# Two tokens per partition for the first pair of a linear-attention and MLP kernel, with its last tile put out in halves and its order drawn anew

## The chip, the core and the metric

The kernel runs on one core of one Trainium2 chip. The metric is the device time of one execution in microseconds (us). A profile is one execution whose instructions were recorded; its span goes from the first to the last instruction and is about 2 us shorter than the execution's time. Each execution also has its mean granted TensorE clock on record, as a share of full speed; in this case that number turned out to sort the runs better than their times do.

Runs are called slow here when they are over 1.5% above the fastest run of the same kernel, and fast otherwise. A run in which the clock fell for a short while can still count as fast by this rule.

## The reference, cut to what matters

```python
def _attn_ref(r, k, v, w, u):            # B=4, H=8, S=768, D=48, float32
    state = np.zeros((B, H, D, D))
    for t in range(S):
        cur = np.einsum('bhd,bhe->bhde', u[None] * kt, vt)
        y[:, :, t] = np.einsum('bhd,bhde->bhe', rt, state + cur)
        state = wt[:, :, :, None] * state + np.einsum('bhd,bhe->bhde', kt, vt)
    return y

def _moe_ref(x, w_in, w_out, s, b):      # 3072 tokens, 384 -> 2048 -> 384
    r = np.maximum(x @ w_in, 0.0)
    return (s * (r * r) + b) @ w_out
# x is y with its heads laid side by side: (B*S, H*D) = (3072, 384)
```

## The kernel before

The kernel cuts each of the four sequences into six chunks of 128 tokens, which gives 24 token tiles n. For each tile the recurrence is turned into matmuls: running sums of log w (`cum`, tile `cums`), their exponentials (`E`), the products of r and k with them (`prd`), a transpose (`trps` to `RK`), the products of all pairs of tokens (`mt_ps`, masked to `mt_sb`), the output `y_ps` (to `x_sb`) and the new state (`d_ps`). Two tiles of `x_sb`, transposed to `xT`, make one MLP tile T of 256 tokens: `h_ps`, a ReLU to `rh`, its square `gT`, then `o_ps`, `o_sb` and the store.

Head by head, one token of one input is 48 numbers, 192 B, in memory. So a load of one tile is 1,024 pieces of 192 B:

```python
    def coords(n):
        return n // B, n % B             # chunk, batch: first the first chunks of the four batches

    def load(n, which):                  # which: 0 w, 1 r, 2 k, 3 v
        cc, bb = coords(n)
        t0 = cc * L                      # L = 128
        # ... (a tile of ain, 8 buffers of each kind)
        nc.sync.dma_start(
            out=dst, in_=src[bb, :, t0 : t0 + L, :].transpose([1, 0, 2])
        )

    def cum(n):
        ps = psA.tile([128, 2, 512], FP32, name="cums", tag="A")    # one buffer, shared with mt_ps
        lw = c["lw"]
        nc.tensor.matmul(ps[:, 0, 0:HD], lhsT=tri_strict, rhs=lw[:, :, 0:D], start=True, stop=True)
        nc.tensor.matmul(ps[:, 1, 0:HD], lhsT=ntri_incl, rhs=lw[:, :, 0:D], start=True, stop=True)
        # ... (four matmuls of one column for the decay of the state)

    def ymm(n):
        ps = psB.tile([128, 512], FP32, name="y_ps", tag="B")       # two buffers
        # ... (four matmuls with the state, if there is one)
        for h in range(H):
            p, sg = divmod(h, 2)
            nc.tensor.matmul(
                ps[:, h * D : (h + 1) * D],
                lhsT=c["mt"][:, sg, p, :],
                rhs=c["vb"][:, h, :],
                # ...
            )

    def g2(T, q):                        # o_ps of the last tile T is taken from psH
        tt, part = divmod(q, 4)
        # ...
        for ft in range(part * 4, part * 4 + 4):
            nc.tensor.matmul(ps, lhsT=gT[T][:, ft, tt * 128 : (tt + 1) * 128],
                             rhs=w_out_sb[ft // FPP][:, ft % FPP, :],
                             start=(ft == 0), stop=(ft == FT - 1))
```

Every instruction stands where a long list puts it; each engine works through its own in that order. `+7` stands for seven warm-up matmuls on zeros (`warm_ps`), which have no use but to keep TensorE busy:

```
load0.0 load0.1 load_u load1.0 load0.2 ln0 load2.0 +13 cum0 load1.1 +1 u_mm exp0 load1.2 u_ev l20
# ...
l22 dmm1 exp3 sup1 rkp3 xev0 +5 mt2 ymm1 mul3 li2 yd1 cd2 +5 tr3 ci0 load4.0 l23 yev1 vb2@P msk2
+6 xtr1 tev3 rku3 lo0 xev1 +7 dmm2 yd2 mt3 cd3 g10.0 sup2 ci1@A li3 msk3 ymm2 g10.1 vb3 relu0.0
# ...
```

In it `li` and `lo` are loads of the pieces of w_in and w_out, `ci` and `co` their casts, `g1` is h_ps, `g2` is o_ps, `tr` and `xtr` are the transposes on TensorE. Tiles from DTK on have r and k, and from DTX on have x, transposed by the DMA instead; from DK2 and DX2 on every second tile has, too.

## Time and profile before

| | before |
|---|---|
| time, median of 3 runs | 192.97 us (192.77 to 193.01) |
| span of the profiled run | 191.46 us, clock 1.00 |
| first h_ps starts | 23.57 us |
| TensorE busy after that | 161.9 us |
| TensorE idle after that | 2.4 us |
| from the last matmul to the end | 3.58 us |

The last four rows add up to the span. They are how the kernel is read in all that follows: a start, in which the first two tiles of attention are made; a dense middle, in which only the amount of TensorE work and its idle time count; and a tail.

Beside the views that the prediction shows, two places of the profile of before are needed later. From its page, the totals of the engines (busy time, share of the span, number of instructions) and one row of the DMA issues (count, KB of each, median us from issue to landing):

```profile
PE 181.7 (95%) x1859; PEld 140.6 (73%) x1859; DVE 125.1 (65%) x188; ACT 143.8 (75%) x272; POOL 105.8 (55%) x131
...
wt<-in_w_dram SPq DMA_DIRECT2D x24, 192.0 KB, 4.4
```

A load of 192 KB lands 4.4 us after it was issued, in the median of 24; its own pieces take only about 1.0 us of that, the pitch at which such loads are issued.

And the last VectorE work in its timeline (start, length, instruction, how many):

```profile
187.27 1.27 DVE L639 SCALAR_TENSOR_TENSOR o_sb<-o_psh,s_bc,bconst 128x384 f32<-128x384 f32 x2 [3.72 <-PE o_psh L629]
```

Both halves of the last MLP tile come to VectorE at nearly the same time, and the second, of 384 columns, ends 0.65 us after the last matmul.

### The profile page before, as it was taken

What the parts mean: (1) busy time and instruction counts of PE and PEld (TensorE: products, weight loads), DVE (VectorE), ACT (ScalarE), POOL (GpSimd) and SP (SyncE); (2) the same over time, 40 slices, a digit from 0 to 9 for tenths busy, and PEclk for the clock granted to TensorE, in tenths of its full rate; (3) what the DMA queues carried; (4) which work ended last, traced back from release to release, by engine and by line L of the source; (5) the groups of instructions that cost most, each with busy time, mean ns of one, the idle gap of its engine ahead of it and who ended that gap; (6) DMA issues with size and microseconds to landing.
All of it is one profiled execution on the core that took longest, in us unless ns stands there. A gap on an engine that the chain in (4) does not pass through costs nothing.

```text
span 191.5 us, 4784 instructions
## 1 busy us (share of the span) xinstructions
PE 181.7 (95%) x1859; PEld 140.6 (73%) x1859; DVE 125.1 (65%) x188; ACT 143.8 (75%) x272; POOL 105.8 (55%) x131
## 2 busy tenths in 40 slices
PE   6987889997999999999999999999999989999992
PEld 4665678875678877787878788888877767888761
DVE  6377784456857938869788697846859597640032
ACT  3756597895879999798869889785695994478910
POOL 3587821516688479799955885546677543100000
PEclk9999999999999999999999999999999999999999
DMA  6999999997999999999999999699999965123022
GB/s 116 197 188 206 312 342 371 238 284 137 189 160 221 184 198 191 187 198 192 222 192 208 178 166 227 145 202 243 177 187 140 203 136 142 25 67 125 0 82 82
DMA packets 124312, 34.75 MB, mean 181 GB/s; under 512 B 119169, under 2 KB 122242, under 8 KB 124290
## 3 DMA queue, kind: packets, MB, share of 16 engines
q1 hardware_dynamic: 124290, 34.45, 92.8%
q8 instruction: 14, 0.23, 0.5%
q14 instruction: 8, 0.07, 0.1%
HBM read 25.17 MB, written 4.72 MB: 156 GB/s over the span
## 4 chain that ended last, share of the span: by engine, by line
PE 63%; SPq 17%; DMA 5%; ACT 4%; issue 4%; DVE 3%; POOL 1%; DVEq 0%
PE h_ps L591 24%; PE o_ps L629 24%; SPq L270 14%; DMA wi_st<-in_moe_w_in_dram 4%; PE mt_ps L427 3%; PE o_psh L629 3%; PE y_ps L464 2%; DMA vt<-in_v_dram 2%; PE d_ps L480 2%; PE y_ps L455 2%; DVE gT L616 1%; PE cums L326 1%; PE cums L329 1%; SPq L696 1%; PE trps L385 1%
## 5 line engine op out<-in xcount | busy, mean ns | idle before, releaser
L591 PE MATMUL h_ps<-xT,w_in 128*128 128x256 bf16 x576 | 77.8, 273 | 0.9 <-DVE w_in L687 0.6
L629 PE MATMUL o_ps<-w_out,gT 128*128 128x384 bf16 x352 | 69.7, 326 | 0.6 <-DVE o_sb L639 0.6
L604 ACT ACTIVATE rh<-h_ps 128x512 bf16<-128x512 f32 x96 | 56.4, 598 | 17.8 <-PE h_ps L591 17.1
L591 PEld LDWEIGHTS <-w_in 128*128 128x128 bf16 x576 | 61.0, 114 | 7.6 <-DVE w_in L687 0.7
L629 PEld LDWEIGHTS <-gT 128*128 128x128 bf16 x384 | 35.5, 98 | 18.4 <-issue 0.6
L614 ACT ACTIVATE gT<-rh 128x512 bf16<-128x512 bf16 x67 | 40.2, 629 | 0.5
L282 POOL TENSOR_TENSOR rkp<-rkt 128x384 f32<-128x384 f32 x24 | 30.3, 1262 | 17.7 <-DMA rkt<-in_k_dram 17.7
L439 DVE TENSOR_TENSOR mt_sb<-mt_ps,tri_strict 128x1024 bf16<-128x1024 f32 x24 | 29.2, 1218 | 9.0 <-PE mt_ps L427 8.9
L358 DVE TENSOR_TENSOR prd<-rkt,E 128x768 bf16<-128x768 f32 x24 | 26.8, 1116 | 7.1 <-DMA rkt<-in_k_dram 5.9
L313 POOL TENSOR_TENSOR yd<-vt,cd 128x384 bf16<-128x384 f32 x24 | 22.0, 916 | 8.4 <-DVE cd L307 8.4
L293 POOL TENSOR_TENSOR rku<-rkp,u_bc 128x384 f32<-128x384 f32 x24 | 25.4, 1060 | 1.9 <-DVE cd L307 1.4
L348 ACT ACTIVATE E<-cums 128x768 bf16<-128x768 f32 x24 | 19.5, 811 | 5.5 <-PE cums L334 3.3
L639 DVE SCALAR_TENSOR_TENSOR o_sb<-o_ps,s_bc,bconst 128x384 f32<-128x384 f32 x22 | 13.3, 610 | 12.8 <-PE o_ps L629 12.4
L494 DVE TENSOR_TENSOR x_sb<-y_ps,yd 128x384 bf16<-128x384 f32 x24 | 13.3, 553 | 11.1 <-POOL yd L313 4.7
L616 DVE TENSOR_TENSOR gT<-rh 128x512 bf16<-128x512 bf16 x29 | 16.8, 594 | 1.9 <-ACT rh L604 1.6
L277 ACT ACTIVATE logw<-wt 128x384 bf16<-128x384 f32 x24 | 12.4, 525 | 5.8 <-DMA wt<-in_w_dram 5.7
L531 POOL TENSOR_TENSOR st<-stmp,l 128x384 bf16<-128x384 bf16 x16 | 14.7, 917 | 2.3 <-DVE stmp L522 2.3
L307 DVE TENSOR_REDUCE cd<-rku 128x8 f32<-128x384 f32 x24 | 13.0, 544 | 3.5 <-POOL rku L293 3.4
L866 PE MATMUL warm_ps<-warm_sb 128*128 128x256 bf16 x84 | 13.2, 295 | 1.1 <-DVE warm_sb L844 1.1
L685 POOL CAST vb<-vt 128x384 bf16<-128x384 f32 x12 | 6.8, 563 | 11.9 <-DMA vt<-in_v_dram 11.9
L400 ACT COPY RK<-trps 128x1024 bf16<-128x1024 bf16 x10 | 10.2, 1016 | 2.7 <-PE trps L385 2.3
L372 POOL TENSOR_TENSOR l<-lam,par 128x8 f32<-128x8 f32 x20 | 6.9, 348 | 8.3 <-ACT lam L352 8.3
(58 smaller groups left out, 168.9 us busy)
## 6 DMA issues: line engine op xcount, KB each, us to landing
wt<-in_w_dram SPq DMA_DIRECT2D x24, 192.0 KB, 4.4
rkt<-in_r_dram SPq DMA_DIRECT2D x24, 192.0 KB, 4.3
rkt<-in_k_dram SPq DMA_DIRECT2D x24, 192.0 KB, 4.3
vt<-in_v_dram SPq DMA_DIRECT2D x24, 192.0 KB, 4.2
out_dram<-o_sb SPq DMA_DIRECT2D x24, 192.0 KB, 2.7
wi_st<-in_moe_w_in_dram SPq DMA_DIRECT2D x4, 768.0 KB, 7.8
wo_st<-in_moe_w_out_dram SPq DMA_DIRECT2D x4, 768.0 KB, 7.6
RK<-prd SPq DMA_TRANSPOSE x14, 4.0
```

The costliest lines, as they stand in the source:

```text
L270: nc.sync.dma_start(out=dst, in_=src[bb, :, t0 : t0 + L, :].transpose([1, 0, 2]))
L282: nc.gpsimd.tensor_tensor(out=rkp, in0=c["rk"][:, 0].rearrange("t h d -> t (h d)"), in1=c["rk"][:, 1].rearrange("t h d -> t (h d)"), op=AL ...
L293: nc.gpsimd.tensor_tensor(out=rku.rearrange("t h d -> t (h d)"), in0=c["rkp"], in1=u_bc, op=ALU.mult)
L313: nc.gpsimd.tensor_tensor(out=yd, in0=c["v"], in1=c["cd"].unsqueeze(2).to_broadcast([128, H, D]), op=ALU.mult,)
L348: nc.scalar.activation(out=E, in_=ps[:, :, 0:HD], func=AF.Exp)
L358: nc.vector.tensor_tensor(out=prd[:, :, :, 0:D].rearrange("t x h d -> t (x h) d"), in0=c["rk"].rearrange("t x h d -> t (x h) d"), in1=c["E ...
L439: nc.vector.tensor_tensor(out=m.rearrange("s g p t -> s (g p) t"), in0=c["mt_ps"].rearrange("s g p t -> s (g p) t"), in1=tri_strict.unsque ...
L591: nc.tensor.matmul(ps[:, f, :], lhsT=w_in_sb[ft // FPP][:, kt, :].rearrange("p (m j) -> p j m", j=FPP)[:, ft % FPP, :], rhs=xT[T][:, kt, : ...
L604: nc.scalar.activation(out=rh, in_=hs[T, i], func=AF.Relu)
L614: nc.scalar.activation(out=g, in_=rh, func=AF.Square)
L616: nc.vector.tensor_tensor(out=g, in0=rh, in1=rh, op=ALU.mult)
L629: nc.tensor.matmul(ps, lhsT=gT[T][:, ft, tt * 128 : (tt + 1) * 128], rhs=w_out_sb[ft // FPP][:, ft % FPP, :], start=(ft == 0), stop=(ft == ...
```

## The change

The intent is to feed the start faster. The first two tiles are now two successive chunks of one batch, 256 tokens, laid two to a partition: partition p holds tokens 2p and 2p+1. Their 2 x 48 numbers of one head lie side by side in memory, so a piece is 384 B, and four loads replace eight. The price is more and smaller matmuls for that pair, as each half of the array now holds a mixture of even and odd tokens. The last token tile is put out in two halves of 192 columns, so that less is left after the last matmul. The order was drawn anew, with fewer buffers for w and v, more tiles transposed by the DMA, and 54 warm-ups in place of 84.

```diff
-VBE = 'AP'
-DTK = 10
-DTX = 18
-DK2 = 10
-DX2 = 12
+VBE = 'P'
+WB = 5
+VB = 6
+PK = 2
+DTK = 9
+DTX = 12
+DK2 = 24
+DX2 = 24
# ... (ORDER: all of it is new; its first lines, cut)
-load0.0 load0.1 load_u load1.0 load0.2 ln0 load2.0 +13 cum0 load1.1 +1 u_mm exp0 load1.2 u_ev l20
+load0.0 load0.2 load0.1 load2.0 load_u ln0 ln1 load3.0 +13 cum0 exp0 load3.1 +8 cum1 l20 mul0
# ...
+    def load2(n, which):
+        _, bb = coords(n)
+        t = ain.tile([128, 2, H, D], FP32, name="pkt", tag="rk")
+        t = t.rearrange("t x h d -> t (x h d)")
+        nc.sync.dma_start(
+            out=t.rearrange("t (h e) -> t h e", h=H),
+            in_=(w, r, k, v)[which][bb, :, 0 : 2 * L, :].rearrange(
+                "h (t s) d -> t h (s d)", s=2
+            ),
+        )
# ... (in cum, for the pair: four matmuls of 384 columns with half masks, eight of one column)
+            for i, (a, b) in enumerate(
+                ((hs_pos if sl == 0 else hi_pos, hs_pos), (hi_neg, hs_neg if sl == 0 else hi_neg))
+            ):
+                for q, (tri, l) in enumerate(((a, l0), (b, l1))):
+                    nc.tensor.matmul(ps[:, i, 0:HD], lhsT=tri, rhs=l[:, :, 0:D],
+                                     start=(q == 0), stop=(q == 1))
# ... (in ymm, for the pair: 64 rows by 64 columns of the array at a time)
+                for h in range(H):
+                    p, sg = divmod(h, 2)
+                    for q in range(2):
+                        nc.tensor.matmul(
+                            ps[rows, h * D : (h + 1) * D],
+                            lhsT=cb[n0 + q]["mt"][rows, sg, p, 64 * (n % 2) : 64 * (n % 2) + 64],
+                            rhs=cb[n0 + q]["vb"][rows, h, :],
+                            # ...
# ... (the last token tile: k = 1 and 2 are its two halves)
+    def part_of(T, k):
+        if T < NT - 1 or k == 0:
+            return k, slice(0, d_model)
+        half = d_model // 2
+        return 1, slice((k - 1) * half, k * half)
```

## The prediction

> **What bounds the kernel now.** I first read the row of forty slices and then the engine totals by stretch, because an average share hides a start that differs from the rest. I cut the stretches where the trace changes character: 23.57 us is the start of the first matmul of the MLP (h_ps), 187.92 us the end of the last matmul.
>
> ```profile
> PE   6987889997999999999999999999999989999992
> PEclk9999999999999999999999999999999999999999
> ```
>
> ```profile
> core 0: us, PE busy (x) PEld busy (x) DVE busy (x) ACT busy (x) POOL busy (x), PEclk, DMA share, GB/s
> 0.00:23.57 23.57, 19.77 (x209) 13.75 (x209) 15.00 (x29) 13.77 (x22) 15.70 (x26) 1.00 1.09 203
> 23.57:50.00 26.43, 24.58 (x240) 19.44 (x236) 16.44 (x26) 21.78 (x41) 9.85 (x11) 1.00 1.01 267
> 50.00:120.00 70.00, 70.00 (x797) 55.39 (x796) 53.57 (x77) 61.13 (x126) 54.41 (x66) 1.00 1.14 194
> 120.00:160.00 40.00, 39.44 (x397) 30.60 (x392) 29.76 (x40) 30.03 (x55) 25.02 (x28) 1.00 1.00 175
> 160.00:187.92 27.92, 27.89 (x232) 21.40 (x230) 9.75 (x18) 17.04 (x31) 0.83 (x1) 1.00 0.21 68
> 187.92:191.50 3.58, 0.00 (x0) 0.00 (x0) 0.62 (x1) 0.00 (x0) 0.00 (x0) 1.00 0.30 110
> ```
>
> The first number after a stretch is its length, the next TensorE's busy time. After 23.57 us TensorE is busy 24.58 + 70.00 + 39.44 + 27.89 = 161.91 of 164.35 us, at full clock: only 2.4 us of idle time are left there. So the span is a sum of four terms: start 23.57, TensorE work 161.9, idle 2.4, tail 3.6; together 191.5. Busy is not peak, so I checked the work with the chain that ended last: six h_ps matmuls follow each other in 0.65 us and four o_ps matmuls in 0.65 us, thus 109 and 163 ns apiece; with 576, 384 and the smaller groups so priced I get 160.6 us. The work is dense.
>
> The waits of TensorE after 23.5 us say what the idle time is:
>
> ```profile
> PE d_ps L480 <- ACT vb L683: 1.0, 1, 1.0
> PE o_ps L629 <- DVE o_sb L639: 0.6, 1, 0.6
> PE h_ps L591 <- DVE w_in L687: 0.6, 1, 0.6
> PE h_ps L591 <- ACT rh L604: 0.3, 1, 0.3
> ```
>
> The first and third are data that came late from memory: the chain puts the first down to 3.35 us of waiting for a transfer of v, and w_in is cast from a weight piece whose transfer the cast awaited for 0.6 us.
>
> What sets the start? TensorE's 84 warm-up matmuls fill the time before it, so its busy share says nothing there. ScalarE's timeline does:
>
> ```profile
> 20.52 1.47 ACT L683 CAST w_in<-wi_st 128x1536 bf16<-128x1536 f32 x1 [1.48 <-DMA wi_st<-in_moe_w_in_dram]
> 21.90 1.00 ACT L400 COPY RK<-trps 128x1024 bf16<-128x1024 bf16 x1
> 22.80 0.48 ACT L557 COPY xT<-xt_ps 128x384 bf16<-128x384 bf16 x1
> ```
>
> The first weight piece lands at about 20.5, then come a cast, an eviction and the second half of xT, which ends at 23.28. The DMA queue is therefore the limit of the first 23 us: load after load of r, k, v, w (192 KB in 1,024 pieces of 192 B) is issued at a pitch of 1.0 us (10.89, 11.93, 12.97 in the queue's timeline), and fourteen of them stand before that weight piece.
>
> **What the Trainium skill says.** "DMA: Bandwidth & Descriptors", section Specifications, gives at least 512 B as the size for line rate, with a read-modify-write below it. The trace's packet records agree only that small pieces are slow: median 15 ns for 192 B, 18 for 256 B, 65 for 1,536 B, 84 for 2,048 B. The two large sizes give 0.037 ns per byte and 8 ns fixed; that line gives 15 at 192 B. There is no extra step below 512 B; a fixed price per piece explains it, and 384 B should take 8 + 14 = 22 ns. "TensorE: Matmul & The Clock Gate", section Part 1, has an idle array fall to half clock after a window of about 3.4 us; the granted clock here is 1.00 throughout, with the warm-ups in. Its section "Wait — 56ns, not 53.3ns?" gives N / 2.4 GHz + 2.5 ns per matmul: 162.5 ns at 384 columns (trace 163), 82.5 at 192.
>
> **The change, part by part.** From the compiled instruction lists I counted what stands before and after the first h_ps.
>
> *Loads.* Eight loads of 192 B pieces become four of 384 B pieces. A group costs 64 x 15 = 0.96 us per engine (pitch 1.0) now, and 64 x 22 = 1.43, say 1.5 us, for twice the bytes. Saved: 8 x 1.0 - 4 x 1.5 = 2.0 us of queue time. But the order changes too. Ahead of the first w_in piece are now all four paired loads (6.0), seven single ones (7.2) and one w_out piece of 768 KB (about 2.0): 15.2 us against 14.4. The piece should land some 0.8 us later, near 21.3. After that the queue is ahead: that w_out piece, and v of the second to fourth tiles, are already in. By w_out's last piece and the loads for tile 5 I expect the queue 1 to 3 us ahead of before.
>
> *Start.* ScalarE has after the piece: cast 1.47 and both halves of xT, 2 x 0.48; then 0.28 until h_ps, as before. 21.3 + 1.47 + 0.96 + 0.28 = 24.0. The other path to it is the recurrence of the pair through the one buffer that cums and mt_ps share: the pair of w lands near 4.5, two logarithms 1.05, four matmuls of 384 columns and eight tiny ones 0.95, Exp 1.0, the same again for the second, then cums of tiles 2 and 3, and three mt_ps with masks of 1.21 each; summed by hand the second mask ends near 18.5, the two y_ps (36 and 36 small matmuls, about 1.1 us each) near 21.2, the last small products near 23.5. Both paths end at 23.5 to 24.0; I take 23.9, 0.3 later than now. The extra TensorE work of the pair (cums, mt_ps and y_ps are roughly doubled) lies here, where 30 warm-ups are dropped to make room, and costs nothing by itself. The new masks (some six small VectorE and eight small GpSimd operations at 0.1 to 0.2 us) are built while the first loads travel.
>
> *TensorE work after the start.* Gone are 8 trps and 9 xt_ps matmuls of 128 columns (one more tile's r/k and three more x are transposed by the DMA) at 56 ns, 0.95 us, and 4 y_ps<-st at 40 ns, 0.16, because the fifth tile now starts a batch. The last token tile is 32 matmuls of 192 columns at 82.5 ns, 2.64 us, for 16 at 163, 2.61. In sum 161.9 - 1.1 = 160.8 us.
>
> *Idle.* The two waits for late data (1.0 + 0.6) should go, as their data come earlier. The new order has its own collisions; the o_sb wait of 0.6 is as likely as before. I allow 1.0 us instead of 2.4.
>
> *Tail.* The last o_sb has 192 columns, not 384; from VectorE's 553 ns at 384 and 1,214 at 1,024, 1.03 ns per column, it is 0.20 us shorter. The last store's eight packets per engine take 36 ns, not 65: 0.23 us. 3.58 - 0.43 = 3.15.
>
> Sum: 23.9 + 160.8 + 1.0 + 3.15 = 188.85 us of span, 2.65 under now; 192.97 - 2.65 = 190.3 us.
>
> **The rivals.** (1) The queue saving reaches the start: the MLP starts 2 us earlier, the time is near 188. For it: queue time is what the start waits on. Against it: the added w_out piece ahead of the first w_in piece takes the saving up, and the one-buffer chain of the recurrence ends at about the same time. (2) Nothing moves: TensorE is a dense 161 us whatever the start does, and the new order swaps old waits for new ones; 192 to 193. For it: each order has been tuned to its loads, only 2.4 us of idle exist, and buffers are fewer (w 8 to 5, v 8 to 6, and the pair's loads take four of the eight r/k slots). Against it: the 1.1 us of transposes and 0.4 of tail are gone by count. (3) ScalarE becomes the bound: in 50 to 120 us it is busy 61.13 of 70. Against it: it loses one RK eviction (1.0), three xT (0.48 each) and two squares (0.63 each), and gains two casts of v (0.5 each): about 2.7 us less. (4) The array falls to half clock, as 30 of the 84 warm-ups are gone: 1 to 3 us lost at the start. Against it: the pair's own matmuls replace them, and no gap of 3.4 us shows in the order.
>
> **Range and chances.** The start is good to 0.7 us either way, the idle time to 1 us, most of it upward; work and tail to 0.2. That gives 189.2 to 191.9 for 8 in 10. A gain of over 2% means under 189.1 us, which needs rival 1 and almost no idle: 0.11. Over 2% slower needs 4 us of new idle: 0.02.
>
> **What would show it.** Right: paired load packets near 22 ns; the first h_ps at 23 to 24.6; no long wait of d_ps for vb near 47 us; TensorE busy about 160.8 us after the start; a tail near 3.15. Wrong: an h_ps start at or before 22 (rival 1), or waits of TensorE above 2 us in sum after the start (rival 2), or a granted clock below 1.00.

## The result, and the profile after

All ratios are computed as the mean time of one kernel's fast runs over that of the other's of the same rounds, so they are not quite the ratios of the medians that stand beside them.

The changed kernel took 193.19 us in the median of six runs (190.17 to 193.79), the kernel before 192.99 (192.77 to 193.84). By the medians nothing happened. But the six runs are not one group. Seven executions of the changed kernel have their clock on record:

| clock | times, us |
|---|---|
| 0.979 to 0.980 | 193.10, 193.28, 193.29, 193.79 |
| 1.000 | 190.17, 190.77, 191.40 |

The ratio of the fast runs is 0.987 (0.983 to 0.992), which is within 2%. The profile fell on a slow run, and so did that of each later repeat of this kernel: there is no profile of a full-clock run of the unaltered changed kernel, only of close relatives.

From the page of the changed kernel: the totals, the busy tenths of TensorE in forty slices, the granted clock in tenths, and a row of the DMA issues, all to be set against those of before. The last row is from the longer list of its DMA issues.

```profile
PE 184.8 (97%) x1916; PEld 143.3 (75%) x1916; DVE 124.2 (65%) x198; ACT 141.0 (74%) x268; POOL 106.0 (55%) x138
...
PE   6998999999999999999999999999999999999992
...
PEclk9999958999999999999999999999999999999999
...
pkt<-in_w_dram SPq DMA_DIRECT2D x1, 384.0 KB, 3.8
...
out_dram<-o_sb SPq DMA_DIRECT2D x2, 96.0 KB, 1.7
```

TensorE has 3.1 us more of busy time, and 57 more instructions with 30 fewer warm-ups. The paired load of w brings twice the bytes and lands 3.8 us after issue; the two halves at the end are stores of 96 KB. The 5 and 8 in the clock's row are new: from slice six, about 24 us, the array ran at half speed. The stretches, cut where the clock changes (length, then busy time and count of TensorE, its weight loads, VectorE, ScalarE, GpSimd; then clock, DMA share, GB/s):

```profile
core 0: us, PE busy (x) PEld busy (x) DVE busy (x) ACT busy (x) POOL busy (x), PEclk, DMA share, GB/s
0.00:9.75 9.75, 7.54 (x37) 4.17 (x37) 4.88 (x21) 3.62 (x6) 4.89 (x20) 1.00 1.02 188
9.75:23.40 13.65, 12.70 (x209) 9.60 (x207) 9.97 (x13) 10.35 (x15) 10.68 (x12) 1.00 1.18 296
23.40:26.24 2.84, 2.84 (x29) 1.92 (x28) 0.97 (x2) 0.96 (x2) 2.63 (x5) 0.50 1.13 306
26.24:30.23 3.99, 3.99 (x31) 3.07 (x29) 3.15 (x7) 1.47 (x3) 2.31 (x3) 0.50 1.04 363
30.23:50.00 19.77, 19.77 (x188) 15.71 (x186) 11.51 (x17) 18.18 (x37) 8.25 (x10) 1.00 0.99 208
```

Half clock holds from 23.40 to 30.23, which is 6.83 us or two windows of 3.413 us. The first h_ps falls into the middle of it, at 26.24. After it TensorE has no idle time at all: in the dip it works, slowly. The 1.00 of the first row is what stood before the first clock record; the matmuls show that the array was in fact at half speed up to 9.75 us, where a sum of 384 columns took 0.32 us from start to start and 0.16 later. In the profile of before full speed began at 4.45.

In the four terms, from this profile: start 26.24, work 161.68, idle 0.00, tail 3.50, together 191.43 (before 191.46). So this run has less idle time and pays it back at the start. TensorE's own timeline in that stretch:

```profile
20.46 0.65 PE L559 MATMUL y_ps<-vb,mt_sb 64*64 64x48 bf16 x16
...
24.98 0.82 PE L598 MATMUL d_ps<-vb,prd 64*128 64x96 bf16 x8
...
26.24 0.63 PE L721 MATMUL h_ps<-xT,w_in 128*128 128x256 bf16 x2
```

The form `64*64` says that this matmul uses 64 rows and 64 columns of the array of 128 x 128. Sixty-four such matmuls, with a moving operand of only 48 columns, fill most of 20.5 to 23.3 us. In the last full window of 3.41 us before the dip the columns streamed fill 64% of the time at full clock; weighted with the part of the array in use (rows times columns of each matmul, over 128 x 128) it is only 23%. This weighted share is called the use of the array below.

The tail has its last VectorE work, of 192 columns:

```profile
187.96 0.42 DVE L776 SCALAR_TENSOR_TENSOR o_sb<-o_ps,s_bc,bconst 128x192 f32<-128x192 f32 x1 [0.24 <-PE o_ps L765]
```

It ends 0.20 us sooner after the last matmul than in before, yet the tail as a whole is 3.50 us, not 3.15.

### The profile page after: what moved, and what is told of

It is laid out like the page before. It is cut to its first block, busy times and chain, and to the rows that moved or that the text cites. A ratio compares the mean times of both kernels' runs of the same rounds, so it can differ in the third digit from the quotient of the medians.

```text
span 191.4 us, 4916 instructions
## 1 busy us (share of the span) xinstructions
PE 184.8 (97%) x1916; PEld 143.3 (75%) x1916; DVE 124.2 (65%) x198; ACT 141.0 (74%) x268; POOL 106.0 (55%) x138
## 4 chain that ended last, share of the span: by engine, by line
PE 93%; DVE 3%; ACT 1%; issue 1%
PE h_ps L721 35%; PE o_ps L765 33%; PE mt_ps L516 4%; PE y_ps L579 2%; PE warm_ps L1048 2%; PE trps L450 2%; PE cums L383 2%; PE cums L386 2%; PE d_ps L611 2%; PE y_ps L570 2%; PE cs_ps L801 1%; PE cums L368 1%; PE xt_ps L672 1%; PE y_ps L559 1%; DVE prd L424 1%
## 5 line engine op out<-in xcount | busy, mean ns | idle before, releaser
L734 ACT ACTIVATE rh<-h_ps 128x512 bf16<-128x512 f32 x96 | 56.8, 598 | 26.9 <-PE h_ps L721 26.0
L765 PE MATMUL o_ps<-w_out,gT 128*128 128x384 bf16 (+1 forms) x400 | 74.7, 320 | 0.0
L527 DVE TENSOR_TENSOR mt_sb<-mt_ps,tri_strict 128x1024 bf16<-128x1024 f32 x22 | 26.8, 1219 | 11.6 <-PE mt_ps L516 11.6
L318 POOL TENSOR_TENSOR rkp<-rkt 128x384 f32<-128x384 f32 x22 | 22.7, 1033 | 12.6 <-DMA rkt<-in_k_dram 12.6
L347 POOL TENSOR_TENSOR yd<-vt,cd 128x384 bf16<-128x384 f32 x22 | 19.3, 882 | 17.9 <-DVE cd L341 14.8
L324 POOL TENSOR_TENSOR rku<-rkp,u_bc 128x384 f32<-128x384 f32 x24 | 28.1, 1178 | 0.4
L424 DVE TENSOR_TENSOR prd<-rkt,E 128x768 bf16<-128x768 f32 x22 | 25.0, 1136 | 2.6 <-ACT E L404 2.2
L776 DVE SCALAR_TENSOR_TENSOR o_sb<-o_ps,s_bc,bconst 128x384 f32<-128x384 f32 (+1 forms) x25 | 14.8, 597 | 10.5 <-PE o_ps L765 10.2
L652 DVE TENSOR_TENSOR stmp<-d_ps,st 128x384 bf16<-128x384 f32 x16 | 8.8, 553 | 6.2 <-PE d_ps L611 3.3
L1048 PE MATMUL warm_ps<-warm_sb 128*128 128x256 bf16 x54 | 10.7, 337 | 1.1 <-DVE warm_sb L1005 1.1
L516 PE MATMUL mt_ps<-RK 48*128 48x128 bf16 x176 | 9.0, 223 | 0.0
```

Of the source, the lines that this page charges most:

```text
L318: nc.gpsimd.tensor_tensor(out=rkp, in0=c["r"], in1=c["k"], op=ALU.mult)
L324: nc.gpsimd.tensor_tensor(out=rku.rearrange("t h d -> t (h d)"), in0=c["rkp"].rearrange("t h d -> t (h d)"), in1=u_bc, op=ALU.mult,)
L347: nc.gpsimd.tensor_tensor(out=yd, in0=c["v"], in1=c["cd"].unsqueeze(2).to_broadcast([128, H, D]), op=ALU.mult,)
L424: nc.vector.tensor_tensor(out=prd[:, :, :, 0:D].rearrange("t x h d -> t (x h) d"), in0=c["rk"].rearrange("t x h d -> t (x h) d"), in1=c["E ...
L516: nc.tensor.matmul(ps[:, sg, p, :], lhsT=c["KT"][pr, p, :], rhs=c["RT"][pr, p, :], start=(p == 0), stop=(p == HP - 1),)
L527: nc.vector.tensor_tensor(out=m.rearrange("s g p t -> s (g p) t"), in0=c["mt_ps"].rearrange("s g p t -> s (g p) t"), in1=(masks[n % 2] if ...
```

## The experiments

The reason to be tested: the slow runs of the changed kernel are those in which the array falls to half clock at the start of the MLP, and without that the sum of the prediction holds. The rivals: the half clock is a bystander, and slow runs come from the transfers; it is the missing warm-ups alone and not the pair's narrow matmuls that bring the dip; and, for the gain, that it comes from the new order, the moved transposes or the last tile, not from the larger pieces. Twelve experiments ran, in three groups on three chips. All gave correct results. The kernel before ran 43, 24 and 20 times beside them, at a clock of 0.996 or more in every run, with means of 193.40, 193.37 and 193.46 us.

The dips, as the stretches of half clock after the start of full speed are called here, lasted 3.413, 6.827 or 10.240 us in the clock records, so one, two or three windows of 3.413 us. One takes 3.413 / 2 / 191 = 0.9% off a run's mean clock. So 0.991, 0.982 and 0.973 stand for one, two and three windows, and the clock of each run shows its dips without a profile. In this table a run has a dip when its clock is 0.991 or less:

| kernel | chip of group | runs | with a dip: mean us | without: mean us |
|---|---|---|---|---|
| changed, first result | | 7 | 4: 193.36 | 3: 190.78 |
| a_again | 1 | 6 | 2: 193.46 | 4: 190.38 |
| a_third | 3 | 14 | 3: 193.05 | 11: 191.62 |
| a_warm | 1 | 22 | 1: 194.47 | 21: 192.24 |
| b_thin | 1 | 14 | 14: 193.44 | 0 |
| b_tail | 1 | 14 | 0 | 14: 193.34 |
| a_init | 2 | 6 | 0 | 6: 191.27 |
| a_best | 2 | 7 | 0 | 7: 191.30 |
| a_192 | 2 | 11 | 5: 194.27 | 6: 193.86 |
| b_early | 2 | 14 | 0 | 14: 193.40 |
| a_init2 | 3 | 7 | 0 | 7: 191.72 |
| a_late | 3 | 6 | 0 | 6: 191.86 |
| b_xbar | 3 | 6 | 1: 197.75 | 5: 196.46 |

Names with a are edits of the changed kernel, with b of the kernel before. And the four terms of each profile:

| profile | start | work | idle | tail | dip, us from the span's start |
|---|---|---|---|---|---|
| before | 23.57 | 161.91 | 2.41 | 3.58 | none |
| changed | 26.24 | 161.68 | 0.00 | 3.50 | 23.40 to 30.23 |
| a_again | 26.05 | 162.03 | 0.53 | 3.48 | 23.23 to 30.06 |
| a_third | 24.77 | 161.93 | 1.69 | 3.51 | 24.37 to 27.78 |
| a_warm | 27.08 | 160.12 | 1.19 | 3.49 | none |
| a_init | 24.15 | 160.39 | 1.63 | 3.48 | none |
| a_init2 | 24.02 | 160.94 | 1.27 | 3.49 | none |
| a_late | 24.40 | 160.75 | 1.02 | 3.49 | none |
| a_best | 24.86 | 160.14 | 2.20 | 3.51 | none |
| a_192 | 26.84 | 160.23 | 2.29 | 3.45 | 11.09 to 14.50 |
| b_thin | 23.95 | 163.57 | 1.00 | 3.56 | 18.53 to 28.77 |
| b_tail | 24.31 | 161.71 | 1.98 | 3.20 | none |
| b_early | 24.47 | 161.54 | 2.62 | 3.56 | none |
| b_xbar | 23.74 | 162.03 | 5.69 | 3.52 | none |

### a_again: the changed kernel once more

No edit; another occasion. The chip of the first result is not on record.

> The changed kernel again, unaltered. Its runs so far fall in two groups: 190.2 and 190.8 us at a mean clock of 1.00, and 193.1 to 193.8 at 0.98, where the profile shows half clock from 23.4 to 30.2 us. Theory W (the array is loaded too thinly between 18 and 23.4 us, and whether that trips the clock depends on where a free-running window falls): both groups appear again, the slow ones some 2.5 to 3 us above the fast ones, each slow one at a clock of about 0.98. Rival C (something about that chip or that moment, not the kernel): on another occasion the slow group is gone or much rarer, or the kernel before shows it too. If a fast run is profiled: first h_ps near 24, TensorE work after it near 160.8, no wait of TensorE after it over 0.5 us, tail near 3.15.

Measured: median 190.59 us, before 193.43, ratio 0.985 (0.982 to 0.988). Two of the six runs were at a clock of 0.980 and 0.982 and took 193.06 and 193.87; four at 0.997 or more took 190.09 to 190.66. So the two groups came again on another occasion, and they go by the clock; in the kernel before, none of the 43 runs of the same rounds was below 0.996.

### a_warm: 22 warm-ups put back near the end of the attention start

```diff
-... rkp2 msk1 +1 tr3 dmm0 ...
+... rkp2 msk1 +8 tr3 dmm0 ...
-... yd1 ymm1 ci0 yev0 small rku2 xtr0 ... +1 xtr1 vb3 xev1 +1 dmm1 l23 li3 +1 dmm2
+... yd1 +3 ymm1 ci0 yev0 small rku2 +3 xtr0 ... +4 xtr1 vb3 xev1 +4 dmm1 l23 li3 +4 dmm2
```

> The changed kernel with 22 more warm-up matmuls between the last cums of the start and the first h_ps: 7 where TensorE waits before the fourth tile's transposes, 3 before the second y_ps of the pair, 3 before its xt_ps, 3 each before three later waits. Theory W: no run falls to half clock; every run is at clock 1.00 and between 190.2 and 191.2 us, the six inside the y_ps stretch costing up to 0.7 us of start. Rival C: the slow group stays, about as often as without the warm-ups (4 of 6). Rival D (a slow run comes of the late start of the clock at the beginning of the program, at 9.75 us instead of 4.4): slow runs stay too, because nothing before 17 us is changed.

Measured: median 192.14 us, ratio 0.994 (0.992 to 0.996). Only one of 22 runs had a dip, but the runs without one took 192.24 in the mean, 1.86 more than the 190.38 of a_again on the same chip. In the profile there is no dip, yet the first h_ps starts at 27.08: between 24.9 and 26.9 us four warm-ups each stand ahead of the second xt_ps, of d_ps and of the next d_ps, and TensorE does them in order. (The profiled run took 193.68 us, 1.4 above that mean, so its start may be later than is usual.) Put there, warm-ups hold the clock in all runs but one and cost 1.9 us in the mean; the dip costs 3.1 in some of the runs.

### b_thin: the kernel before with 28 of its 84 warm-ups taken out

```diff
-... yev0 +5 cum3 ... xev0 +5 mt2 ... cd2 +5 tr3 ... msk2 +6 xtr1 ... xev1 +7 dmm2
+... yev0 cum3 ... xev0 mt2 ... cd2 tr3 ... msk2 xtr1 ... xev1 dmm2
```

> The kernel before with 31 of its 84 warm-up matmuls taken out, all of them between 15.5 and 23 us; no work is changed. Theory W: some runs fall to half clock near 20 to 27 us, mean clock 0.98 and 2 to 3 us longer (near 195.5), the others stay at 193. Rival C: all runs stay at 193.0 and clock 1.00, like the kernel before. Rival E (it is the narrow 64-row, 48-column matmuls of the pair that fail to count, not the missing warm-ups): also 193.0, as the kernel before has no such matmuls.

The edit takes out 28 (5 + 5 + 5 + 6 + 7); the 31 of the text on record was miscounted. Measured: median 193.5 us, ratio 1.000 (0.997 to 1.003). All fourteen runs had a dip. Its stretches around it:

```profile
15.10:18.53 3.43, 1.69 (x24) 1.21 (x22) 1.86 (x4) 2.42 (x4) 2.27 (x5) 1.00 0.77 154
18.53:23.95 5.42, 3.56 (x40) 2.36 (x39) 4.14 (x6) 3.41 (x6) 4.32 (x6) 0.50 1.07 325
```

The window before the dip is half empty (1.69 of 3.43 us), and then half clock lasts for three windows. There are no narrow pair matmuls in this kernel, so the missing warm-ups alone are enough for a dip; that the narrow matmuls must be there is refuted. But the dip cost nothing that shows in the times, 193.44 us in the mean against 193.40: in the profile the start is 0.38 us later, work after it rose by 163.57 - 161.91 = 1.66 us, and idle time fell by 2.41 - 1.00 = 1.41. The slow matmuls ran where TensorE had been waiting for data.

### b_tail: only the last tile's two halves, in the kernel before

```diff
-... store10.0 g211.5 g211.2 g211.6 g211.3 g211.7 oev11.0 store11.0 oev11.1 store11.1
+... store10.0 g211.2 g211.3 oev11.0 store11.0 g211.5 g211.6 g211.8 g211.7 oev11.1 store11.1 g211.9 g211.10 g211.11 oev11.2 store11.2
# and part_of, g2, oevac and store as in the change
```

> The kernel before with only the end changed: the last token tile in two halves of 192 columns. My sum: tail 3.15 us instead of 3.58 (last o_sb 0.42 instead of 0.62, last store 0.23 shorter), the work unchanged (32 x 82.5 ns for 16 x 163): 0.4 us faster, ratio 0.998. Rival: the store's time is its landing latency, so only the 0.2 us of o_sb come; or the narrower matmuls are paced by their weight loads at about 100 ns, which would give back 0.55 us and leave it level or slower.

Measured: median 193.36 us, ratio 1.001 (0.999 to 1.003). The tail in the profile is 3.20 us in place of 3.58, as expected, but no time came of it that could be measured; the run-to-run spread of the kernel before at full clock is 0.6 us (standard deviation of its 43 runs), and 0.4 should still have shown in the ratio's interval. By the interval the halves alone are worth 0.15% at the most. The rival of the weight loads falls: the last 32 matmuls of 192 columns follow each other in 82.5 ns in the median.

### a_init: five more warm-ups at the very start

```diff
-load0.0 load0.2 load0.1 load2.0 load_u ln0 ln1 load3.0 +13 cum0 exp0 ...
+load0.0 load0.2 load0.1 load2.0 load_u ln0 ln1 load3.0 +18 cum0 exp0 ...
```

> The changed kernel with 18 warm-up matmuls instead of 13 at the very beginning; they fill the stretch from 4.0 to 5.2 us in which TensorE waits for the first logarithms. Both profiles of the changed kernel have half clock until 9.6 to 9.8 us, so the pair's cums matmuls of 384 columns are spaced by 0.32 us, not 0.16. Theory S (this cold beginning delays the pair's recurrence): full clock begins before 8 us in every profile, and the first h_ps comes 0.7 to 1.5 us earlier than the 26.1 us of the slow profiles; the fast group stays at 190.2 or a few tenths below. The dip at 23.4 us is not treated, so a slow group some 3 us above stays (W). Rival: the beginning is hidden behind the loads, and nothing moves.

Measured: six runs from 190.94 to 191.46 us, all at a clock of 0.996 or more; ratio 0.989 (0.987 to 0.992). The slow group that was expected to stay did not appear. This is the nearest thing to a profile of the changed kernel at full clock. Its stretches:

```profile
0.00:24.15 24.15, 21.95 (x275) 15.28 (x276) 15.88 (x36) 14.82 (x23) 16.70 (x34) 1.00 1.12 253
24.15:50.00 25.85, 24.66 (x250) 19.85 (x247) 16.10 (x24) 21.51 (x43) 12.24 (x15) 1.00 1.00 242
50.00:120.00 70.00, 69.80 (x775) 55.23 (x776) 54.36 (x79) 59.53 (x120) 50.98 (x63) 1.00 1.02 185
120.00:160.00 40.00, 39.76 (x391) 30.76 (x389) 28.23 (x39) 30.71 (x57) 22.54 (x25) 1.00 1.05 189
160.00:186.17 26.17, 26.17 (x240) 20.96 (x237) 11.28 (x22) 14.59 (x26) 1.80 (x3) 1.00 0.28 76
```

After 24.15 us TensorE is busy 24.66 + 69.80 + 39.76 + 26.17 = 160.39 us and idle 1.63. And TensorE's timeline, to be set against that of the changed kernel above:

```profile
19.25 0.65 PE L559 MATMUL y_ps<-vb,mt_sb 64*64 64x48 bf16 x16
...
23.43 0.50 PE L598 MATMUL d_ps<-vb,prd 64*128 64x96 bf16 x8
...
24.15 0.60 PE L721 MATMUL h_ps<-xT,w_in 128*128 128x256 bf16 x4
```

The same y_ps starts at 19.25 in place of 20.46, and from it to the first h_ps it takes 4.90 us in place of 5.78. So the time that the slow run loses has three parts: 1.21 us at the beginning, where the array came to full speed only at 9.75 (here at 6.87); 0.88 before the first h_ps, in the dip; and 161.68 - 160.39 = 1.29 us more work after it. Against these stand 1.63 us of idle time that vanished, and 0.02 of tail: 191.43 - 189.65 = 1.78 us of span in all. With a_again the same sum gives 1.90 + 1.64 - 1.10 = 2.44.

ScalarE's timeline of the same run shows the two paths to the start meet (the bracket is idle time before, and what ended it):

```profile
21.53 1.47 ACT L825 CAST w_in<-wi_st 128x1536 bf16<-128x1536 f32 x1 [0.69 <-DMA wi_st<-in_moe_w_in_dram]
22.91 0.85 ACT L687 COPY xT<-xt_ps 128x384 bf16<-128x384 bf16 x2
```

### a_best: that, and 13 of the warm-ups of a_warm

```diff
-... load3.0 +13 cum0 ... msk1 +1 tr3 ... yd1 ymm1 ... rku2 xtr0 ...
+... load3.0 +18 cum0 ... msk1 +8 tr3 ... yd1 +3 ymm1 ... rku2 +3 xtr0 ...
```

> The 18 warm-ups of a_init, and 13 of those of a_warm: 7 more before the fourth tile's transposes, where TensorE waits 0.8 us, 3 before the pair's second y_ps and 3 before its xt_ps; the nine between the later small products, which held up the start in a_warm (first h_ps at 27.1), are left out. Theory W with S: no dip, no slow group: all runs between 190.2 and 191.3, the mean below the 191.9 of the twelve runs of the changed kernel so far. Rival: the six warm-ups inside the y_ps stretch cost as much as the dip (0.7 us on all runs against 3 on half of them would still be a gain), or the load of 18 to 24 us is still too thin and a slow group stays.

Measured: median 191.30 us, ratio 0.988 (0.985 to 0.991), no dip in seven runs, mean 191.30 against 191.27 of a_init. The extra warm-ups add nothing.

### a_192: the changed kernel with pieces of 192 B

```diff
-        nc.sync.dma_start(
-            out=t.rearrange("t (h e) -> t h e", h=H),
-            in_=(w, r, k, v)[which][bb, :, 0 : 2 * L, :].rearrange("h (t s) d -> t h (s d)", s=2),
-        )
+        for i in range(2):
+            nc.sync.dma_start(
+                out=t[:, :, i, :],
+                in_=(w, r, k, v)[which][bb, :, 0 : 2 * L, :].rearrange("h (t s) d -> s t h d", s=2)[i],
+            )
```

Everything else, order, masks, halves and transposes, stays; only the four paired loads are eight again, of 1,024 pieces of 192 B.

> The changed kernel with the descriptors alone undone: two tokens per partition still, but each of the four paired loads goes out as two loads of 1,024 pieces of 192 B. Queue time by the packets of the two profiles: 1,024 pieces of 384 B took 1.5 us, of 192 B 1.04, so 4 x (2.09 - 1.5) = 2.4 us more before the first weight piece of w_in, and 0.6 us more before the pair's w. Theory R (the start is set by the pair's recurrence, not by the weight piece): the start moves by 0.6 to 1.2 us, and the fast group by as much, to about 191. Rival Q (the start follows the queue): 2.4 us, to 192.5. Rival N: slack everywhere, no change.

Measured: median 194.09 us, ratio 1.005 (1.001 to 1.008): slower than the kernel before. Five of its eleven runs had a dip, but the six without took 193.86 in the mean, 2.59 more than a_init on the same chip at the same clock. That is close to the 2.4 us of the rival Q. The profiled run starts its first h_ps at 26.84, 2.69 later than a_init, and has one dip, long before, at 11.09 to 14.50. That this dip is not what made the start late can be seen on ScalarE, to be set against the cast at 21.53 of a_init above:

```profile
24.22 1.47 ACT L826 CAST w_in<-wi_st 128x1536 bf16<-128x1536 f32 x1 [0.64 <-DMA wi_st<-in_moe_w_in_dram]
```

The cast waits for the weight piece here too, and begins 2.69 us later, as much as the first h_ps: the queue sets the start. So the larger pieces are worth the whole gain of the change: all its other parts together, without them and in an order that was drawn for them, come to 193.86 / 193.37 = 1.003 of the kernel before.

### b_early: one load of the kernel before moved up

```diff
-... mul4 load5.1 g20.5 ... sq1.4@A load4.3 g11.6 ...
+... mul4 load4.3 load5.1 g20.5 ... sq1.4@A g11.6 ...
```

This moves the load of v for which d_ps waited 1.0 us in the kernel before.

> The kernel before with one load moved: v of the fifth tile is issued before r and k of the sixth instead of five loads later. In its profile TensorE waits 0.98 us at 46.9 us for the cast of that tile. If an idle microsecond of TensorE after the start is a microsecond of the time (the sum of my prediction), the wait goes and the median falls by 0.7 to 1.0 us (192.5 against 193.4). Rival: the wait moves to the sixth tile, whose r and k now come 1 us later, and the time stays.

Measured: median 193.31 us, ratio 0.999 (0.996 to 1.001). That wait is gone; TensorE's waits between 23 and 60 us in the profile, of a run of 194.40 us, 1.0 above the mean, begin with these (us in total, times, longest):

```profile
PE cs_ps L659 <- DVE w_out L687: 1.5, 1, 1.5
PE cums L326 <- ACT logw L277: 0.5, 1, 0.5
```

The last piece of w_out, right behind which the moved load now stands in the queue, is cast at 43.35 in place of 41.51, and the next w is late too. (In b_tail, where no load was moved, that cast is at 42.41, so about half of the delay may be the run's own.) Idle time after the start is 2.62 us, not less than 2.41. In this profile the load moved forward only named another one to wait for. It fits a stream of loads that bounds up to some 50 us, but one profile does not show it.

### a_third and a_init2: both once more, side by side

No edit to the changed kernel, and a_init again.

> The changed kernel a third time, on the same chip and in the same rounds as a_init2 and a_late. So far six of its twelve runs lie at 190.1 to 190.8 and six at 193.1 to 193.9. Theory W: again two groups, near 190.4 and 193.4. A profile of a fast run, if there is one: no half clock after the first 10 us, first h_ps near 24.5, start and idle time of TensorE together near 25.4. Rival: on this chip only one group, then the two-group picture depended on the chip or the moment.

> The changed kernel with 18 instead of 13 first warm-ups, again, beside a_third. Before, six runs at 190.9 to 191.5 with no slow group. Theory W+S (full clock early, then the recurrence is over before the thin stretch meets a whole window, so no dip): one group again near 191.3; mean 0.5 to 1 us below the mean of a_third, but 0.8 above its fast group. Rival: the six were luck, and a slow group near 194 appears.

Measured: a_third has a median of 191.79 us and a ratio of 0.991 (0.988 to 0.994), a_init2 191.51 and 0.991 (0.988 to 0.994). Three of fourteen runs of a_third had a dip (193.68, 193.56 and 191.92), none of seven of a_init2. On this chip the two groups are less clean: full-clock runs of a_third reach from 190.80 to 192.72, and one of a_init2 took 193.14 at a clock of 1.00. Without the runs with a dip a_third is at 191.62 and a_init2 at 191.72, so at full clock the five warm-ups cost and gain nothing. Both expectations were missed: the full-clock runs of a_third lie 1.2 us above the 190.4 that was expected, and the mean of a_init2 is only 0.2 below that of all runs of a_third (191.93), not 0.5 to 1. In the profile of a_third the array was at full speed from 3.89 us on, and there was a dip all the same: a late rise of the clock at the beginning isn't needed for it.

All in all the changed kernel had a dip in 9 of 27 runs, and its three variants with the five warm-ups at the start, a_init with its repeat, a_best and a_late, in none of 26. That they spare the dip is well supported by the counts; on the one chip where both ran it is 3 of 14 against 0 of 13, which could be chance.

### a_late: a_init with one transpose put later

```diff
-... yev4 tr6 msk5 g21.1 ln8 load7.3 yd5 tev6 g21.5 st3 ...
+... yev4 msk5 g21.1 ln8 load7.3 yd5 g21.5 tr6 tev6 st3 ...
```

In a_init the longest wait after the start is one of 1.1 us of trps for prd, at 49.1.

> a_init with one more edit: the transposes of the seventh tile (trps), for which TensorE waits 1.08 us at 49.1 in the profile of a_init (r and k of that tile come late), are put behind the next two groups of o_ps matmuls (1.3 us of work whose data are there). If that wait is a microsecond on the path: 190.2 to 190.5, a version better than both. Rival, as in b_early: what comes behind waits for the same stream of loads, and the time stays at 191.3.

Measured: median 191.73 us, ratio 0.992 (0.988 to 0.995), mean 191.86 against 191.72 of a_init2: no gain. The experiment does not test what it was made for: the wait at 49.1 is gone from the profile, but it is absent from that of a_init2 as well, which is a_init unedited. (The waits of trps that are left in both, of 0.6 us at the most, lie before the first h_ps.) Idle time after the start is 1.02 us, against 1.27 in a_init2.

### b_xbar: only the moved transposes, in the kernel before

```diff
-DTK = 10
-DTX = 18
-DK2 = 10
-DX2 = 12
+DTK = 9
+DTX = 12
+DK2 = 24
+DX2 = 24
# and the words tr9, xtr12, xtr14 and xtr16 taken out of the order, where it is else unchanged
```

> The kernel before with only the transposes moved: one tile's r and k (8 trps matmuls) and three tiles' x (9 xt_ps matmuls) go to the DMA. By the sum of the prediction 17 x 56 ns = 0.95 us of TensorE work after the start; all of it lies after 55 us, where TensorE has hardly an idle moment. Theory: TensorE busy after the first h_ps 160.9 to 161.0 instead of 161.9, median 0.9 us down, ratio near 0.995. Rival: the order was laid for the transposes on TensorE, so a new wait for a transpose of the DMA (4 us to landing) takes it back, ratio 1.000.

Measured: median 196.96 us, ratio 1.017 (1.012 to 1.021): 3 us slower, which is worse than the rival expected. Idle time after the start is 5.69 us. Three of TensorE's waits over the whole span:

```profile
PE d_ps L480 <- ACT vb L683: 1.7, 2, 1.0
PE cums L326 <- ACT lam L352: 1.2, 1, 1.2
...
PE h_ps L591 <- DMA xT<-x_sb: 0.9, 2, 0.7
```

The first is hardly longer than in the kernel before, where the same view has 1.6; the second and third are new. With the old order TensorE waits for the transposed tile itself (the third line). And the busy time after the start is 162.03 us, where 160.9 to 161.0 was expected: 17 matmuls are gone, and no busy time with them. So in this order handing the transposes to the DMA saved nothing; that the new waits all come of the queue is not shown.

## Why the prediction was right or wrong

That the time would stay within 2% was right, and at full clock the range was; what the median would be was wrong, since the prediction didn't see that the kernel would have two groups of times. The 18 full-clock runs of the changed kernel have means of 190.78, 190.38 and 191.62 us on three occasions, and 14 of the 18 lie in the range 189.2 to 191.9; all seven of the first two do. The seven runs at 0.979 to 0.982 are at 193.06 to 193.87, above it, and four of them decide the median of the first result, 193.19. How close 190.3 came to the first two means is in part luck: in a_init, whose terms are known, start, idle and tail were 1.2 us larger than predicted and the work 0.4 smaller, and its runs took 191.27.

**The step that failed.** It is the dismissal of the fourth rival: "the pair's own matmuls replace them, and no gap of 3.4 us shows in the order". There was indeed no gap, and the array fell to half clock all the same, in 9 of 27 runs; "a granted clock below 1.00" stands among the prediction's own signs of being wrong. In the five windows of 3.41 us that came just before a dip, in the profiles of the changed kernel, its two repeats, b_thin and a_192, the use of the array was 0.20 to 0.34; in no window of before, up to 31 us, was it under 0.55. (Nor was the clock of before "1.00 throughout", as the prediction reads it: its matmuls ran at half speed up to 4.45 us, ahead of the first clock record.) I had treated busy as yes or no, for a stretch that I myself had filled with matmuls of 64 by 64 and 48 columns. The size, "1 to 3 us", was right: runs with and without a dip differ by 2.6 us in the first result, 3.1 in a_again and 1.4 in a_third, where two of the three dips had one window only, and the profiles of the first two give 1.8 and 2.4 against a_init. That the dip causes the difference, and doesn't only go with it, rests on the terms of the profiles, which name where each part of it lies, and on the variants without a dip; no experiment switched the clock alone.

**Start: right at full clock.** Predicted 23.9; a_init, a_init2 and a_late start at 24.15, 24.02 and 24.40. The paths met as written: in a_init the cast of the first w_in piece begins at 21.53, after a wait for its transfer, where the landing was put at 21.3, and the first half of xT is copied at 22.91, right when that cast is done. The first three groups of 1,024 pieces of 384 B took 1.4 to 1.9 us each, 1.5 predicted; but the median piece took 25 to 28 ns and not 22. The line that gave 22 had less under it than was written: in before the records of 1,536 B are the stores (24 x 128 = 3,072 of 3,073), and those of 256 B are pieces of the DMA's transposes (14 x 1,024 + 9 x 384 = 17,792, all that there are), not loads.

**The first rival, and where the queue's saving went.** I wrote that the added w_out piece "takes the saving up", as if the larger pieces bought nothing at the start. a_192 puts it better: without them the first piece of w_in comes 2.7 us later, and the first h_ps with it. The saving is what keeps the start where it was and brings the later data forward: the fifth tile's v is cast at 43.71 us in a_init, but at 47.10 in a_192, as in before (47.12). It isn't a small term beside others; it is the gain.

**Work: right.** 160.8 predicted; 160.39, 160.94 and 160.75 measured in those three.

**Idle: right in size, not in its reason.** Predicted 1.0 us, with the two waits for late data gone; measured 1.63, 1.27 and 1.02, and the wait of d_ps near 47 us is gone. But b_early, in which it is gone too, was no faster, so such a wait wasn't shown to be a cost of its own. In its place the new order has another wait of d_ps, for GpSimd's cast of v near 130 us: 0.2 us in a_init, but 1.5 in a_third, the kernel unaltered, out of 1.69 us of idle time.

**Tail: mis-sized by 0.35.** Predicted 3.15 us, measured 3.45 to 3.51 in all profiles of the changed kernel and its edits. The two terms of the step were right: the last o_sb ends 0.20 us sooner, and SyncE's wait for the last store ends 2.12 us after the last matmul in place of 2.58. What follows that wait, the closing steps on the engines, took 1.38 us in place of 1.00; 0.30 of the difference lies between two of GpSimd's last steps. It isn't the halves, as b_tail has 3.20 with the same wait. Oddly, the part of the execution outside the span went the other way: 2.2 us for the kernel before and all its edits (193.68 - 191.46 in the profiled run), 1.8 for the changed kernel and all its edits (191.44 - 189.65 in a_init). The two about cancel; what moved them stays open.

**The second and third rivals fell.** The full-clock runs gain 1.8 to 3.0 us, so it isn't true that nothing moves; and ScalarE was busy 59.53 of 70 us in a_init between 50 and 120, 1.6 less than before, and TensorE's waits of over 0.2 us after the start name VectorE and GpSimd there.

What stays open: what exactly makes the clock fall. Every profiled dip came after a window with a low use of the array, but in a_late a window of 0.22 and in a_warm one of 0.26 passed without, and others of 0.32 to 0.36 in a_192, a_init and a_init2. And the windows aren't tied to the start of the kernel: each dip began a whole number of them after the array came to full speed (4, 4 and 6 in the changed kernel and its repeats), which was anywhere from 3.89 to 9.75 us. Why five warm-ups in the first four us should spare a dip at 23 us, the runs don't tell. Nor is there a version that clearly beats the changed kernel: a_init has the same time at full clock, and gains only by not having the slow runs.

## What to carry to other kernels

Before taking warm-up matmuls away, look at how much of the array the remaining matmuls use in each window of some 3.4 us, not at whether TensorE is busy; and look at the clock of every run, since a median over two groups tells of neither. Where many small loads stand in one queue ahead of the first result, join their pieces first, as that saving moved the first weight piece by 2.7 us here; a single load put further forward, or transposes handed to the DMA under an old order, gained nothing. And price a half-clock stretch against the idle time that it fills: here dips cost nothing that shows in one kernel and 1.4 to 3.1 us in another.

## What the Trainium skill lacked or had wrong

- "TensorE: Matmul & The Clock Gate", section "Why this matters for your kernels", has "No PE-idle gaps >~3µs between matmul bursts" as the way to avoid drops in the middle of a kernel. It isn't enough: the changed kernel had no idle time of TensorE in the 3.4 us before its dip and fell to half clock, when its matmuls used 0.23 of the array. The page doesn't say how narrow matmuls count. Nor is the use of the array the whole rule, as windows of 0.22 and 0.26 passed without a dip in two other profiles.
- The same page, section Part 1, gives the window as 3413 ns and free-running. The runs agree: dips lasted 3.41, 6.83 and 10.24 us, one, two and three times that, and began at different places of the same kernel (23.40, 23.23 and 24.37). It also says that the phase makes runs of one kernel differ, and puts the penalty of the rise at the start under 1% of a typical span, with which the runs agree as far as they go (1.21 us of 191 between a rise at 9.75 and one at 6.87). What it lacks is a fall later on that comes in some runs of a kernel and not in others, and with it two groups of times, here 190.4 and 193.5 us on one chip, 1.6% apart; that the phase decides between them is not shown.
- "DMA: Bandwidth & Descriptors", section Specifications, has 512 B as the least size for line rate, with a read-modify-write below. The runs can't test the limit, as no load had pieces between 384 and 2,048 B. They show a fixed price a piece: two pieces of 192 B took 30 ns in the median, one of 384 B 25 to 28, and groups of 1,024 took 2 x 1.04 us against 1.4 to 1.9. The page's section on small descriptors names such a price, but gives no times of a piece by size, which would help, since here that was the whole gain.
- "Runtime: NRT & Kernel Launch" lists steps before and after a kernel, but nothing that tells why the closing steps took 1.00 us in one kernel here and 1.38 in the other, or why the time outside the span was 2.2 and 1.8 us.
